# What SyncE waits for at the end of a gated attention and SSM kernel: every transfer's semaphore, or only those not known to have landed

## The chip, the cores and the metric

One Trainium2 chip, one NeuronCore of it. The time is the device time of one execution in microseconds (us); less is better. The profile is of one execution on that core. The engines are TensorE (PE in the profile, its weight loads PEld), VectorE (DVE), ScalarE (ACT), GpSimd (POOL) and SyncE (SP). SyncE does no arithmetic here: it issues transfers (DMAs) and waits on semaphores. Every engine has an instruction queue of its own, and the engines meet only through semaphores.

## What is computed

Two branches work on the same input of 2048 tokens by 512 channels and are mixed by a gate for each token. Branch A is an attention with a compressive memory over four segments of 512 tokens, with 32 heads of 16; branch B is a diagonal state-space layer, a causal convolution of length 2048 for each channel, written with FFTs.

```python
x = A_x
g = _sigmoid((x * gate_w).sum(-1, keepdims=True))
a = _A_ref(x, A_wq, A_wk, A_wv, A_wo, A_beta)
b = _B_ref(x, B_A_re, B_A_im, B_B_re, B_B_im, B_C_re, B_C_im, B_log_dt, B_Dskip)
return g * a + (1 - g) * b
```

The output is 2048 x 512 in bf16, 2 MB.

## The kernel before

The kernel is a graph of operations (`Op`), each with an engine, what it reads and what it writes. A fixed list, `ORDER`, says in which order they are put into the queues; `Sched.replay` walks this list and gives each operation its place `pos` in it, and `Sched.emit` turns it into instructions. At the end of the graph `final(s, tb)` runs 16 times, for four segments of four blocks of 128 tokens. It multiplies the attention's result by the output weights in PSUM, adds the state-space branch on VectorE (line 1389), and sends 128 x 512 values to the output. These 16 transfers are the last ones that SyncE issues.

`emit` works out which waits are needed. The names that matter:

- `dsem` is the list of semaphores for transfers. `NDMA` is 150; GpSimd issues nine transfers, which is not over 20, so `nhw` is 150 - 30 = 120 semaphores for the queues of SyncE and ScalarE, used in turn (`k = nd % nhw`), and nine more, one for each transfer of GpSimd: 129. A transfer adds 16 to its semaphore when it has landed.
- `duse[k]` is the last transfer so far on semaphore `k`, and `dcnt[k]` the number of transfers on it.
- `know` is what an engine can be sure of when it has waited: for each semaphore the highest count that it knows to be reached. An operation starts with what its engine knew (`last[o.eng]`). It waits for another operation only when that isn't known already, and with every wait it takes over all that the other operation's engine knew at that point (`d.know`). `last[e]` keeps the result for the engine's next operation. After the walk, `last["SP"]` is what SyncE knows behind its last transfer.
- `make(e)` writes an engine's queue. For SyncE it appends a loop behind the last transfer (lines 336 to 339): a wait for each semaphore that was ever used, in the order of their numbers, until its full count. All engines then meet at the end of the block (line 1436 in the profile).

The loop doesn't run on the chip: it writes one wait after the other into the program, and the compiler forms instructions from them. In the profile they are the `EVENT_SEMAPHORE` instructions of line 339.

Of the kernel before, what the change touches and what calls it, by code (L numbers as in the profile page):

```python
# [98 lines left out]
class Sched:  # L99
# [164 lines left out]
    def emit(self):  # L264
        nc, es = self.nc, self.es
        sems = {e: es.enter_context(nc.semaphore("q_" + e)) for e in ("PE", "ACT", "DVE", "POOL")}
        npool = sum(o.isdma for o in self.prog["POOL"])
        nhw = NDMA - npool if npool > 20 else NDMA - 30
        dsem = [es.enter_context(nc.semaphore("d%d" % i)) for i in range(nhw + npool)]
        block = es.enter_context(nc.Block())  # L270
        duse = [None] * len(dsem)
        dcnt = [0] * len(dsem)
        nd = nsw = 0
        last = {e: {} for e in self.prog}
        for o in self.order:
            know = dict(last[o.eng])
            o.waits = []
            deps = {id(d): d for d in o.alld}
            if o.isdma:
                if o.eng == "POOL":  # L280
                    k = nhw + nsw
                    nsw += 1
                else:
                    k = nd % nhw
                    nd += 1
                if duse[k] is not None:
                    deps[id(duse[k])] = duse[k]
                duse[k] = o
                dcnt[k] += 1
                o.sem, o.val = ("D", k), dcnt[k]  # L290
            else:
                o.sem, o.val = o.eng, o.idx
            o.inc = False
            for d in sorted(deps.values(), key=lambda d: -d.pos):
                assert d.pos < o.pos
                if d.eng == o.eng and o.eng == "PE":
                    continue
                if know.get(d.sem, 0) >= d.val:
                    continue
                o.waits.append(d)  # L300
                d.inc = True
                for kk, vv in d.know.items():
                    if know.get(kk, 0) < vv:
                        know[kk] = vv
            last[o.eng] = know
            o.know = dict(know)
            o.know[o.sem] = max(o.know.get(o.sem, 0), o.val)
        cum = {}
        for e, lst in self.prog.items():
            n = 0  # L310
            for o in lst:
                if not o.isdma and o.inc:
                    n += 1
                cum[id(o)] = n

        def tok(d):
            if d.isdma:
                return dsem[d.sem[1]], 16 * d.val
            return sems[d.eng], cum[id(d)]

        def make(e):
            def run(eng):
                for o in self.prog[e]:
                    need = {}
                    for d in o.waits:
                        s, v = tok(d)
                        if id(s) not in need or need[id(s)][1] < v:
                            need[id(s)] = (s, v)
                    for s, v in need.values():
                        eng.wait_ge(s, v)  # L330
                    ins = o.fn(eng)
                    if o.isdma:
                        ins.then_inc(dsem[o.sem[1]], 16)
                    elif o.inc:
                        ins.then_inc(sems[e], 1)
                if e == "SP":
                    for k in range(len(dsem)):
                        if dcnt[k]:
                            eng.wait_ge(dsem[k], 16 * dcnt[k])
            return run  # L340
        with nc.allow_low_precision("bf16 kernel by design"):
            block.sync(make("SP"))
            block.tensor(make("PE"))
            block.scalar(make("ACT"))
            block.vector(make("DVE"))
            block.gpsimd(make("POOL"))
# [1135 lines left out]
```

## Time and profile before

| | |
|---|---|
| runs of the kernel before | 301.18, 306.3, 302.49 us |
| their median | 302.49 us |
| the profiled execution | 302.64 us |
| its span, first to last instruction | 300.8 us |
| mean granted TensorE clock in it | 0.985 |
| busy in the span: PE, VectorE, ScalarE | 264.5, 267.1, 261.2 us |
| transfers issued to the output | 16, of 128 KB each |

The span is shorter than the execution's own time by 1.8 us. Rows of one line of the kernel read so: line, engine (a q behind it is the engine's instruction queue), operation and tiles, the count, the shortest, median and longest duration in ns, and the start of the first and the last in us from the span's start. With a window, only the instructions inside it are counted. An instruction that waits for a semaphore has its start where the wait is over, so that the time it waited stands as a gap before it. "DMA to landing" is the time from a transfer's issue to the semaphore's last increment.

### The profile page before, as it was taken

To read this page: it belongs to the slowest core of one execution; us is meant where nothing else is said; L and a number is where in the kernel's file an instruction comes from. 1 tells how busy PE (TensorE), PEld (TensorE's weight loads), DVE (VectorE), ACT (ScalarE), POOL (GpSimd) and SP (SyncE) were. 2 spreads that over 40 slices of the span, in tenths; PEclk is the share of its full clock that TensorE was granted. 3 is DMA by queue.
4 is the path that set the end of the run, shared out by engine and by line. 5 is a ranking of instruction groups with operands and counts; after the bars stand their busy time and mean duration, and the time that the engine had idled before them with its cause. 6 is when DMAs were issued, how large, how long until landed. Compare 5 with 4: busy or idle time off the path is not lost.

```text
span 300.8 us, 10359 instructions
## 1 busy us (share of the span) xinstructions
PE 264.5 (88%) x4358; PEld 185.1 (62%) x4395; DVE 267.1 (89%) x651; ACT 261.2 (87%) x307; POOL 7.8 (3%) x18
## 2 busy tenths in 40 slices
PE   5768677987898989999899889999999999998990
PEld 3434344564556656677666666777766887886540
DVE  2799999989999899989999987999899988969881
ACT  4998999999999999969999989899989899988300
POOL 7000000000010000000000000000000000000000
PEclk9997999999999899999999999999999999999998
DMA  6963364433226535464755568776778777557652
GB/s 157 300 196 97 107 137 128 107 91 89 77 79 176 141 69 172 135 182 125 233 160 167 153 186 245 207 221 208 209 228 224 240 219 228 149 152 197 190 181 68
DMA packets 58865, 49.89 MB, mean 166 GB/s; under 512 B 19569, under 2 KB 54274, under 8 KB 58818
## 3 DMA queue, kind: packets, MB, share of 16 engines
q1 hardware_dynamic: 58096, 48.71, 56.3%
q8 instruction: 35, 0.57, 0.9%
q0 software_dynamic: 288, 0.21, 0.5%
q10 hardware_dynamic: 434, 0.30, 0.4%
q14 instruction: 12, 0.10, 0.1%
HBM read 28.88 MB, written 8.39 MB: 124 GB/s over the span
## 4 chain that ended last, share of the span: by engine, by line
PE 46%; ACT 31%; DVE 8%; DMA 7%; issue 5%; SPq 0%; ACTq 0%
PE psum L699 45%; ACT sb L1095 15%; ACT sb L226 10%; DMA sb<-c_DNM 3%; ACT sb L826 3%; DMA sb<-sb 2%; DMA sb<-in_A_x_dram 2%; DVE sb L227 1%; DVE sb L1389 1%; DVE sb L1327 1%; ACT sb L973 1%; DVE sb L1195 1%; DVE sb L1198 1%; DVE sb L1107 1%; PE psum L970 1%
## 5 line engine op out<-in xcount | busy, mean ns | idle before, releaser
L699 PE MATMUL psum<-sb 128*128 128x17 bf16 (+10 forms) x4224 | 255.2, 225 | 26.9 <-ACT sb L1095 11.5
L699 PEld LDWEIGHTS psum<-sb 128*128 128x128 bf16 (+5 forms) x4261 | 175.4, 99 | 102.5 <-issue 20.9
L1095 ACT ACTIVATE sb<-psum 128x2048 bf16<-128x2048 f32 x80 | 151.9, 1899 | 7.3 <-PE psum L699 6.2
L226 ACT ACTIVATE sb<-psum 128x512 bf16<-128x512 f32 (+3 forms) x162 | 94.7, 640 | 13.9 <-PE psum L699 13.0
L227 DVE CAST sb<-psum 128x512 bf16<-128x512 f32 x60 | 40.9, 691 | 7.1 <-PE psum L699 6.9
L1198 DVE TENSOR_TENSOR sb<-sb 128x512 bf16<-128x512 bf16 (+3 forms) x44 | 24.1, 549 | 1.2 <-PE psum L699 1.0
L1202 DVE TENSOR_TENSOR sb<-sb 128x512 bf16<-128x512 bf16 (+3 forms) x44 | 24.0, 551 | 0.5
L1195 DVE TENSOR_TENSOR sb<-sb 128x512 bf16<-128x512 bf16 (+3 forms) x44 | 24.0, 551 | 0.2
L1107 DVE TENSOR_TENSOR sb<-sb 128x1024 bf16<-128x1024 bf16 (+1 forms) x40 | 22.4, 573 | 1.7 <-ACT sb L1095 1.4
L1327 DVE TENSOR_TENSOR sb<-sb 128x1024 bf16<-128x1024 bf16 x32 | 21.7, 682 | 2.4 <-DMA sb<-sb 2.4
L1070 DVE TENSOR_TENSOR sb<-psum,sb 128x256 bf16<-128x256 f32 x32 | 13.4, 418 | 0.5
L826 ACT ACTIVATE sb<-sb 128x512 f32<-128x512 f32 x18 | 11.9, 659 | 0.1
L1389 DVE SCALAR_TENSOR_TENSOR sb<-sb,psum 128x512 bf16<-128x512 bf16 x16 | 11.1, 742 | 0.9 <-PE psum L699 0.5
L1235 DVE TENSOR_TENSOR sb<-sb 128x2048 bf16<-128x2048 bf16 x8 | 9.4, 1212 | 0.0
L1230 DVE TENSOR_TENSOR sb<-sb 128x4096 bf16<-128x4096 bf16 x4 | 9.1, 2281 | 0.0
L1067 DVE RECIPROCAL sb<-psum 128x16 f32<-128x16 f32 x32 | 7.8, 246 | 1.1 <-PE psum L699 1.1
L1147 DVE TENSOR_TENSOR sb<-psum,sb 128x512 bf16<-128x512 f32 x12 | 8.3, 688 | 0.3
L973 ACT ACTIVATE sb<-psum 128x512 bf16<-128x512 bf16 x12 | 7.4, 624 | 1.1 <-PE psum L970 1.1
L827 DVE TENSOR_TENSOR sb<-sb 128x256 f32<-128x256 f32 x18 | 7.5, 419 | 0.2 <-ACT sb L826 0.2
L1024 ACT ACTIVATE sb<-sb 128x512 bf16<-128x512 bf16 x12 | 7.4, 627 | 0.2 <-PE psum L699 0.2
L828 DVE SCALAR_TENSOR_TENSOR sb<-sb 128x256 f32<-128x256 f32 x18 | 7.5, 415 | 0.0
L835 DVE CAST sb<-sb 128x512 bf16<-128x512 f32 x17 | 7.1, 417 | 0.0
(77 smaller groups left out, 113.8 us busy)
## 6 DMA issues: line engine op xcount, KB each, us to landing
sb<-c_DNM SPq DMA_DIRECT2D x32, 320.0 KB, 3.7
sb<-c_DNM SPq DMA_DIRECT2D x32, 192.0 KB, 3.4
sb<-sb SPq DMA_DIRECT2D x84, 64.0 KB, 3.0
scr_Z<-sb SPq DMA_DIRECT2D x16, 256.0 KB, 2.4
sb<-scr_Z SPq DMA_DIRECT2D x32, 128.0 KB, 3.1
sb<-sb SPq DMA_DIRECT2D x32, 128.0 KB
sb<-in_A_x_dram SPq DMA_DIRECT2D x4, 512.0 KB, 5.3
scr_C<-sb SPq DMA_DIRECT2D x8, 256.0 KB, 3.3
```

The source lines that it names most:

```text
L226: fa = lambda e: e.activation(dst(), src(), ACT.Copy)
L227: fd = lambda e: e.tensor_copy(dst(), src())
L699: mm = lambda e, o_, l, r_, st, sp, **kw: e.matmul(o_, lhsT=l, rhs=r_, start=st, stop=sp, skip_group_check=True, **kw)
L826: op("ACT", ("As", 512), lambda e, sq=sq, Z=Z: e.activation(ap(sq, n=512), ap(Z, n=512), ACT.Square), r=[Z], w=[sq], key=PW[h] + PWS * k)
L1070: op("DVE", ("V1", 256), lambda e: e.tensor_tensor(ap(o1, gi * 16, [[128, 4], [32, 4], [1, 16]]), ap(T, dims=[[68, 4], [17, 4], [1, 16]]), ...
L1095: o = op("ACT", ("Ax", 2048), lambda e, P=P, pT=pT: e.activation(ap(pT, n=2048), ap(P, n=2048), ACT.Exp, scale=0.25), r=[P], w=[pT])
L1107: op("DVE", ("V2", 128 * nb), lambda e, pT=pT, dims=dims: e.tensor_tensor(ap(pT, dims=dims + [[1, 128]]), ap(pT, dims=dims + [[1, 128]]), ...
L1195: op("DVE", ("V2" if n > 1 else "V1", 256 * n), lambda e: e.tensor_tensor(run(tile, ne, dst, 1), run(tile, ne, src, sstep), zz(cl * 512), ...
L1198: op("DVE", ("V2" if n > 1 else "V1", 256 * n), lambda e: e.tensor_tensor(run(t2, n, 0, 1), run(tile, ne, src, sstep), zz(cl * 512 + 256), ...
L1202: op("DVE", ("V2" if n > 1 else "V1", 256 * n), lambda e: e.tensor_tensor(D_(), D_(), ap(t2, n * 128, [[-n * 128, 2], [2 * n, 64], [1, 2 * ...
L1327: op("DVE", ("V2", 1024), lambda e, Y=Y, XAB=XAB, K3=K3: e.tensor_tensor(ap(Y, dims=[[512, 2], [1, 512]]), ap(XAB, dims=[[512, 2], [1, 512 ...
L1389: op("DVE", ("V1", 512), lambda e: e.scalar_tensor_tensor(ap(ou, n=512), ap(CTT[s], tb * 512, n=512), ap(omgT, 4 * s + tb, n=1), ap(P, n=5 ...
```

## The change

Behind SyncE's last transfer, the loop over the semaphores is changed in two ways. It goes through them in the order of the place of the last transfer on each (`duse[k].pos`), the oldest first, with unused semaphores ahead (-1); and it writes a wait only where what SyncE knows, `last["SP"]`, is less than the full count of that semaphore. The old test, `dcnt[k]` not zero, is contained in the new one, since an unused semaphore has a count of 0 and 0 is not less than 0.

```diff
                 if e == "SP":
-                    for k in range(len(dsem)):
-                        if dcnt[k]:
+                    for k in sorted(range(len(dsem)), key=lambda k: duse[k].pos if duse[k] else -1):
+                        if last["SP"].get(("D", k), 0) < dcnt[k]:
                             eng.wait_ge(dsem[k], 16 * dcnt[k])
```

Nothing else is changed: the order of the operations, the semaphores that each transfer uses, and all waits ahead of the loop are the same.

## The prediction

> **What bounds the kernel now.** The page comes first, for the span and for what its last part holds: its head, the clock row of the forty slices and the engines' shares of the chain that ended last.
>
> ```profile
> span 300.8 us, 10359 instructions
> PEclk9997999999999899999999999999999999999998
> PE 46%; ACT 31%; DVE 8%; DMA 7%; issue 5%; SPq 0%; ACTq 0%
> ```
>
> The body is a chain through TensorE and ScalarE, and the change touches none of it. The shares add up to 97%; of the rest, the chain's last piece and a table of stretches at the end show the larger part. In the table each row is a stretch, its length, the busy time of PE, weight loads, VectorE, ScalarE and GpSimd with instruction counts, the granted TensorE clock, the DMA share and the GB/s.
>
> ```profile
> 293.97 0.75 DVE sb L1389
> 290.00:294.80 4.80, 3.88 (x18) 1.57 (x16) 4.41 (x7) 0.00 (x0) 0.00 (x0) 1.00 0.52 172
> 294.80:297.00 2.20, 0.00 (x0) 0.00 (x0) 0.00 (x0) 0.00 (x0) 0.00 (x0) 1.00 0.33 110
> 297.00:299.00 2.00, 0.00 (x0) 0.00 (x0) 0.00 (x0) 0.00 (x0) 0.00 (x0) 0.93 0.02 4
> 299.00:300.80 1.80, 0.00 (x0) 0.00 (x0) 0.00 (x0) 0.00 (x0) 0.00 (x0) 0.50 0.00 0
> ```
>
> The last arithmetic ends at 293.97 + 0.75 = 294.7 us. From there to 300.8 no engine computes: 6.1 us, 2% of the span. Until about 297 data still moves; after that almost nothing does. So the last stretch is neither arithmetic nor transfer, and the views of SyncE's queue have to tell what it is: all output transfers, the last one alone with its time to landing, the waits at line 339 (the loop that the change edits), and who was waited for there (total us, times, longest).
>
> ```profile
> L222 SPq DMA_DIRECT2D out_dram<-sb x16: 332/333/594, 284.0 to 294.7; - x16
> ...
> L222 SPq DMA_DIRECT2D out_dram<-sb x1: 333/333/333, 294.7 to 294.7; - x1
> ...
> DMA to landing us min/median/max: 1.7/1.7/1.7
> ...
> L339 SPq EVENT_SEMAPHORE  x64: 27/28/28, 295.1 to 300.4; - x64
> L339 SPq EVENT_SEMAPHORE  x5: 28/28/28, 295.1 to 295.6; - x5
> L339 SPq EVENT_SEMAPHORE  x59: 27/28/28, 296.5 to 300.4; - x59
> ...
> SPq L339 <- DMA out_dram<-sb: 1.0, 2, 0.8
> ```
>
> The loop became 64 instructions. Two for each would make 128 semaphores; that they hold two each is my reading of 64 against the 129 that the code allots (150 - 30, and one for each of nine GpSimd transfers), the odd one going with the branch behind the loop. Five begin by 295.6. Then SyncE stands still until 296.5, which is when the last transfer, issued at 294.7 and 1.7 us on its way, lands at 296.4; the waits view confirms that output transfers are the only thing SyncE ever stood for here, twice, 1.0 us in all. The sixth instruction therefore is the wait for the last transfer. The 58 behind it wait for transfers that landed long before, and pass at the speed of the queue until 300.4. Nothing else runs then, so they lie bare on the end of the kernel.
>
> **The change part by part.** *What is removed.* The pitch of a wait that doesn't stop comes from a stretch in which all pass, and one irregular place stands in three narrow windows.
>
> ```profile
> L339 SPq EVENT_SEMAPHORE  x33: 28/28/28, 298.0 to 300.0; - x33
> ...
> L339 SPq EVENT_SEMAPHORE  x2: 28/28/28, 297.3 to 297.4; - x2
> nothing on L339; most used: []
> L339 SPq EVENT_SEMAPHORE  x3: 28/28/28, 297.8 to 297.9; - x3
> ```
>
> 33 in 2.0 us is 0.061 us each, twice the 28 ns of the record. 58 x 0.061 = 3.5 us. Between 297.4 and 297.8 SyncE issued nothing: 0.4 us, 0.3 more than a pitch. Together 3.8 us; the difference of first and last start, 300.4 - 296.5 = 3.9, agrees. I take 3.9, because it needs no model of the pitch. It all lies on the path: the end of the program waits for SyncE, as the rows of the block's end show.
>
> ```profile
> L1436 SPq COMPARE_BRANCH  x1: 41/41/41, 300.4 to 300.4; - x1
> L1436 SPq DRAIN  x1: 13/13/13, 300.6 to 300.6; - x1
> L1436 POOLq EVENT_SEMAPHORE  x2: 17/17/17, 300.7 to 300.7; - x2
> L1436 PEldq EVENT_SEMAPHORE  x1: 51/51/51, 300.8 to 300.8; - x1
> ```
>
> Branch, drain, GpSimd's signal and the release of the others follow the loop in 0.4 us, with nothing between; they move forward with it and stay as long.
>
> [...]
>
> *What stays.* The new list holds a semaphore only if SyncE's own bookkeeping hasn't seen its last value. Each wait hands SyncE everything that the engine it waited for knew, and the waits ahead of the last outputs are on VectorE's line 1389, the last step of every chain; so loads that any engine consumed are known. The 16 output transfers are waited for by nobody, so they stay: 16 semaphores, some 8 instructions. I can't see the bookkeeping in the trace, so the count is bounded: 16 from below, all 129 from above. It costs nothing up to a point: SyncE reaches the loop at 295.1 and the last transfer lands at 296.4, and 1.3 us at 0.061 is 21 instructions, 42 semaphores, hidden by the transfer's flight. I take 16, by the row of the 16 outputs and the lack of any other waiting at line 339. Should the cover go, because the list is longer, each pair more costs 0.061 us.
>
> *What moves.* The list is now in order of issue, so the newest output is its end. The compiler may pair the list otherwise; if the wait for the newest came first of eight, seven would follow it, 7 x 0.061 = 0.4 us. If last, none. I take none, for before it was one of the middle of the numbers that came early, and now nothing in the list is newer; 0.4 stays for the range. No transfer is moved, no wait is added, and the queues of GpSimd, ScalarE, VectorE and TensorE get the same instructions; what SyncE issues up to 294.7 is the same too.
>
> *What is late next.* The flight of the last transfer, 1.7 us behind the last addition. It isn't touched.
>
> Sum: the profiled execution took 302.64 us, its span 300.8, with 1.8 outside it that I leave as they are. 302.64 - 3.9 = 298.7; the median of the runs shown, 302.49, is 0.15 below that execution, so the median would be 298.6 to 298.7. New span: 296.9.
>
> **The rivals.** *A fetch behind the branch.* The gap of 0.4 us at 297.4 looks like SyncE waiting for instructions, and one block of instructions was moved in that tail, as the row of the queue between 297 and 300.8 us shows.
>
> ```profile
> q14 instruction: 1, 0.01, 0.9%
> ```
>
> In the changed kernel the branch comes at 296.5, ahead of both. If the code behind the branch isn't there yet, SyncE waits at the branch instead: 0.3 us as in the gap gives 302.64 - 3.6 = 299.0; as long as an output's whole flight, 1.7 us, gives 302.64 - 2.2 = 300.4. Against it: from branch to drain took 0.2 us before, and SyncE stands for nearly a second microsecond at the last transfer, in which a fetch can go on. [...]
>
> *The list isn't short.* If nearly all 129 stay, 64 instructions run from 295.1 without the stop, 64 x 0.061 = 3.9, plus the 0.3 gap, to 299.0 or 299.3; the branch was at 300.4, so 1.1 to 1.4 us are gained: 301.2 to 301.5. For it: nothing in the trace shows the list. Against it: the merging of what each engine knows, above.
>
> *The tail isn't in the measured time, or something of the same length stands behind it.* Then 302.6. Against it: 302.64 and the span differ by only 1.8 us, less than the tail's 3.9, so at least 2.1 of it is counted.
>
> *Slower: stretches at half clock.* Two stretches of the body ran at a granted clock of 0.50, and in the second the chain was on TensorE.
>
> ```profile
> 22.23:25.63 3.40, 3.18 (x11) 1.05 (x8) 3.35 (x11) 3.17 (x4) 0.00 (x0) 0.50 0.47 112
> 97.32:100.72 3.40, 3.25 (x108) 2.18 (x108) 2.32 (x10) 2.88 (x5) 0.00 (x0) 0.50 0.59 148
> 97.28 3.31 PE psum L699 x61
> ```
>
> Such a stretch costs up to half its 3.4 us, 1.7. The tail itself ended at 0.50, idle; a program shorter by 3.9 us starts and ends elsewhere in whatever steps the throttle counts. If the body caught more of them, in the thin stretches beside 22 and 97 us, it would decide from three on: 3 x 1.7 = 5.1 against 3.9, and 298.7 + 5.1 = 303.8. The runs shown, 301.18 to 306.3, differ by just about three. Against it: nothing ties the place of the windows to the tail, and the same instructions at the same distances feed TensorE.
>
> **How the numbers follow.** The forecast, 298.7, has 0.75. The fetch has 0.12 (299.0 to 300.4), the long list 0.06 (301.2 to 301.5), no gain 0.04, slower 0.03. The likeliest case gives the number: 298.7. The range goes down by one half-clock stretch, 298.7 - 1.7 = 297.0, which is also close to the fastest run shown less the gain (301.18 - 3.9 = 297.3), and up to 301.4, through the fetch and into the long list, and over a median that is drawn up by one or two disturbed bodies; left out are no gain, slower, and bodies beyond one stretch. What a measurement of this kernel tells from no change is about 2%, 6 us; the whole bare tail is 3.9, 1.3%, so the gain itself stays within it. Faster by over 2% (under 296.4) needs the tail and two stretches at half clock less, 7.3 us: 0.05. Slower by over 2% (over 308.5) needs six stretches more: 0.02. The rest, 0.93, is within.
>
> **What would show it.** Right: eight or so instructions at line 339, the last beginning when the last output lands, 1.7 us behind its issue; the branch one pitch later; the span ending some 0.5 us behind that landing; the stretch before 294.8 as it was. Wrong list: more than 21 instructions there. Wrong order: several instructions behind the landing. Fetch: a gap between branch and drain of over 0.2 us, or an instruction transfer inside it. Wrong altogether: landing and end as close as that and the time still 302, which would put the tail outside what is measured, or a granted clock row with more low slices.

## The result and the profile after

The changed kernel took 300.29 us, the median of 20 runs (296.87 to 304.84); beside it the kernel before took 304.17 us in 20 runs (300.42 to 309.34). The ratio is 0.9879, with a 95% interval from 0.9839 to 0.9918: 3.7 us less, 2.5 to 4.9 by the interval. All ratios in this document leave out the runs that took over 1.5% longer than the fastest of the same kernel. The difference of the medians, over all 20 runs each, is 3.9 us. The profiled execution of the changed kernel took 298.33 us against 302.64, its span 296.4 against 300.8.

Lines of the page, and then of the views of line 339, of the last output transfer, of the waits of SyncE from 290 us on, and of the block's end, all of the changed kernel:

```profile
span 296.4 us, 10298 instructions
...
PEclk9999999999999999999999999999999999999999
...
q14 instruction: 11, 0.09, 0.1%
```

```profile
L339 SPq EVENT_SEMAPHORE  x3: 17/28/28, 294.7 to 296.0; - x3
...
L222 SPq DMA_DIRECT2D out_dram<-sb x1: 332/332/332, 294.3 to 294.3; - x1
...
DMA to landing us min/median/max: 1.7/1.7/1.7
...
SPq L339 <- DMA out_dram<-sb: 1.2, 2, 0.6
...
L1436 SPq COMPARE_BRANCH  x1: 41/41/41, 296.0 to 296.0; - x1
L1436 SPq DRAIN  x1: 13/13/13, 296.2 to 296.2; - x1
```

61 of the 64 wait instructions are gone, and the count of recorded instructions fell by as many, 10359 - 10298. The last output is issued at 294.3 and lands 1.7 us later, at 296.0; the last of the three waits begins at 296.0, the branch one pitch behind it, the drain 0.2 us behind that, and the span ends at 296.4. The stretches at the end show the same from the side of the engines (stretch, its length, busy PE, weight loads, VectorE, ScalarE and GpSimd, clock, DMA share, GB/s):

```profile
294.20:296.00 1.80, 0.00 (x0) 0.00 (x0) 0.03 (x1) 0.00 (x0) 0.00 (x0) 1.00 0.44 148
296.00:296.40 0.40, 0.00 (x0) 0.00 (x0) 0.00 (x0) 0.00 (x0) 0.00 (x0) 1.00 0.00 0
```

Where 3.8 us passed without arithmetic and with hardly any data before (297.0 to 300.8), 0.4 are left. By the unrounded starts of the trace, the end of the span comes 2.18 us behind the issue of the last output, and came 6.10 us behind it before: 3.92 us. The two spans differ by 4.40 us. The other 0.5 us lie ahead of the last issue, where both kernels run the same instructions, and are of the kind by which runs of one kernel differ: in a second profile of the changed kernel the last output is issued 1.2 us earlier than in this one.

### The profile page after: what moved, and what is told of

Its sections match the earlier page's. It is cut to its first block, busy times and chain, and to the rows that moved or that the text cites. A ratio compares the mean times of both kernels' runs of the same rounds, so it can differ in the third digit from the quotient of the medians.

```text
span 296.4 us, 10298 instructions
## 1 busy us (share of the span) xinstructions
PE 264.6 (89%) x4358; PEld 185.4 (63%) x4395; DVE 266.9 (90%) x651; ACT 261.1 (88%) x307; POOL 7.8 (3%) x18
## 4 chain that ended last, share of the span: by engine, by line
PE 35%; ACT 29%; DVE 15%; DMA 10%; issue 7%; SPq 2%; ACTq 0%; DVEq 0%
PE psum L699 35%; ACT sb L1095 14%; ACT sb L226 9%; DMA sb<-sb 5%; DVE sb L227 3%; ACT sb L826 2%; SPq L222 2%; DMA sb<-in_A_x_dram 2%; DMA sb<-c_DNM 2%; DVE sb L1389 2%; DVE sb L1327 1%; DMA out_dram<-sb 1%; DVE sb L1195 1%; DVE sb L1198 1%; ACT sb L973 1%
```

## The experiments

One distance carries the readings: from the issue of the last output to the end of the span. It leaves out the body, whose time moves by several us from run to run, and it repeats closely: the two profiles of the changed kernel give 2.18 and 2.17 us. All values of it are from the unrounded starts of the traces. The traces also list the semaphores of each instruction: a wait instruction holds two of them, the first only one where the count is even, and one is left for the branch behind the loop. So 6 semaphores make 3 wait instructions, and 129 make 64.

| kernel | semaphores waited for at the end | wait instructions | last issue to end, us | ratio to before (95%) |
|---|---|---|---|---|
| before | 129, by number | 64 | 6.10 | 1 |
| changed | 6, by age | 3 | 2.18 | 0.9879 (0.9839 to 0.9918) |
| sort alone | 129, by age | 64 | 5.09 | 0.998 (0.9939 to 1.0021) |
| list of 36 | 36, by age | 18 | 2.35 | 0.9833 (0.9742 to 0.9924) |
| waits ahead of the outputs | 6, by age | 3 | 2.17 | 0.9883 (0.9831 to 0.9936) |
| loop twice | 258, by number | 129 | 9.02 | 1.0142 (1.0082 to 1.0203) |
| 15 output buffers | 15, by age | 7 | 2.18 | 0.9867 (0.9808 to 0.9925) |
| changed, again | 6, by age | 3 | 2.17 | 0.9885 (0.9814 to 0.9956) |

**The sort alone.** The filter is taken out, the order stays.

```diff
-                        if last["SP"].get(("D", k), 0) < dcnt[k]:
+                        if dcnt[k]:
```

> All 129 semaphores are waited for again, but in order of age. Theory (only waits that begin after the last output has landed cost time): the 64 wait instructions run without a stop from 0.4 us behind the issue of the last output, 64 x 0.061 us and one gap of 0.3, so the end comes 0.4 + 3.9 + 0.3 + 0.5 = 5.1 us behind that issue, where it was 6.1 before the change and 2.2 with it; the time is about 1.0 us below before. Rival (the list's length alone decides): 6.1 us, the time as before. Rival (the order does the work of the change): 2.2 us, 3.9 below before.

Line 339, the last output, and two narrow windows on line 339:

```profile
L339 SPq EVENT_SEMAPHORE  x64: 27/28/28, 295.7 to 300.0; - x64
...
L222 SPq DMA_DIRECT2D out_dram<-sb x1: 332/332/332, 295.3 to 295.3; - x1
...
DMA to landing us min/median/max: 1.7/1.7/1.7
...
L339 SPq EVENT_SEMAPHORE  x3: 28/28/28, 296.9 to 297.3; - x3
nothing on L339; most used: []
```

5.09 us, as the theory had it, and neither the 6.1 nor the 2.2 of the rivals. The newest output is now the last in the queue, and it has landed at 297.0 while SyncE is still at the older ones: the stop of 0.8 us that the kernel before had at its sixth wait is gone. So the flight of the last output hides the waits that run before it lands, 20 of them here (the twentieth begins at 296.95), and those that run after the landing are bare, even though they stand ahead of the wait for that output. The time moved by 0.2%, and the interval holds both the expected 1.0 us and none, but not 3.9. The last window, from 297.0 to 297.3, is empty: the gap of 0.4 us is here too, after the twentieth wait as before.

**A list of 36.** The loop of the change, with the 36 semaphores used last.

```diff
-                    for k in sorted(range(len(dsem)), key=lambda k: duse[k].pos if duse[k] else -1):
-                        if last["SP"].get(("D", k), 0) < dcnt[k]:
+                    for k in sorted(range(len(dsem)), key=lambda k: duse[k].pos if duse[k] else -1)[-36:]:
+                        if dcnt[k]:
```

> The changed loop with 36 semaphores, the 36 that were used last, 30 of them long known to have landed: 18 wait instructions in place of 3. Theory (the flight of the last output hides up to 21 of them): the end 2.2 us behind the issue of the last output, as with the change, and the time 3.9 below before. Rival (each wait costs its 0.061 us wherever it stands): 2.2 + 15 x 0.061 = 3.1 us, 3.0 below before.

Line 339, the last output, and the steps of the block's end in this execution:

```profile
L339 SPq EVENT_SEMAPHORE  x18: 17/28/28, 297.2 to 298.6; - x18
...
L222 SPq DMA_DIRECT2D out_dram<-sb x1: 332/332/332, 296.9 to 296.9; - x1
...
DMA to landing us min/median/max: 1.7/1.7/1.7
...
L1436 SPq DRAIN  x1: 13/13/13, 298.8 to 298.8; - x1
...
L1436 DVEq EVENT_SEMAPHORE  x1: 21/21/21, 299.0 to 299.0; - x1
L1436 PEldq EVENT_SEMAPHORE  x1: 51/51/51, 299.0 to 299.0; - x1
L1436 SPq EVENT_SEMAPHORE  x1: 17/17/17, 299.2 to 299.2; - x1
```

The eighteenth wait begins at 298.6, when the output of 296.9 lands: fifteen more waits moved it by nothing, so the rival falls. Yet the distance is 2.35, 0.17 more than with the change, and the rows say where: all engines are released at 299.0, SyncE itself only at 299.2, 0.4 us behind its drain instead of 0.16. In the kernel before, in the sort alone, with the loop twice and with the waits ahead of the outputs, SyncE's gap of 0.4 us always lies between the same two of its recorded instructions, the 335th and the 336th. In this kernel these are the drain and SyncE's last step. The times, of four runs, are too few to tell 3.9 us from 3.0.

**The same waits in another place.** The change stays, and waits for the 128 semaphores whose counts SyncE knows by then (those that the outputs use again, up to the use before) are put ahead of the first output transfer. 126 of them make 63 wait instructions.

```diff
                 for o in self.prog[e]:
+                    if e == "SP" and o is self.prog["SP"][-16]:
+                        for (d, k), v in sorted((x, v) for x, v in o.know.items() if isinstance(x, tuple) and x != o.sem):
+                            eng.wait_ge(dsem[k], 16 * v)
```

> The loop of the change at the end, and the waits that it leaves out put ahead of the first output transfer, where SyncE stood idle for 5.5 us in the profile of before: as many instructions as before the change, in another place. Theory (the place decides): they take about 4 us of the idle time there, the first output is issued when it was, the end comes 2.2 us behind the issue of the last output, and the time is 3.9 below before. Rival (the instructions cost what they cost, by their number and by having to be fetched): the time as before, the 4 us appear ahead of the outputs.

The head of the page, the added waits (line 326 of this kernel), the waits at its end (line 342) and its outputs, all and the last:

```profile
span 296.6 us, 10399 instructions
...
L326 SPq EVENT_SEMAPHORE  x63: 27/28/178, 277.7 to 282.1; - x63
...
L342 SPq EVENT_SEMAPHORE  x3: 17/27/28, 294.8 to 296.1; - x3
...
L222 SPq DMA_DIRECT2D out_dram<-sb x16: 332/384/1705, 283.6 to 294.4; - x16
...
L222 SPq DMA_DIRECT2D out_dram<-sb x1: 333/333/333, 294.4 to 294.4; - x1
```

63 waits take 4.4 us, from 277.7 to 282.1, where SyncE has nothing to do, and the first output goes out at 283.6 (284.0 before, 283.3 with the change). With 64 instructions more in SyncE's queue than the changed kernel has (385 recorded against 321), the span is 296.6 against 296.4, and the ratio to before is that of the change, 0.9883 against 0.9879. The number of instructions costs nothing here; their place does.

**The loop twice.** The kernel before, with its loop run two times.

```diff
-                    for k in range(len(dsem)):
-                        if dcnt[k]:
-                            eng.wait_ge(dsem[k], 16 * dcnt[k])
+                    for h in range(2):
+                        for k in range(len(dsem)):
+                            if dcnt[k]:
+                                eng.wait_ge(dsem[k], 16 * dcnt[k])
```

> The loop of before, gone through twice: 258 semaphores, 129 wait instructions. The wait for the newest output stands only behind some 70 others, so nothing stops. Theory: 0.4 + 129 x 0.061 + 0.3 (a gap, perhaps two) + 0.5 = 9.1 to 9.4 us from the issue of the last output to the end, against 6.1: 3.0 to 3.3 us more time than before. Rival (no wait is hidden by the flight): 6.1 + 65 x 0.061 = 10.1 us, 4.0 more. Rival (the tail lies outside the measured time): a longer tail in the profile, the time as before.

The loop (line 340 of this kernel) and its last output:

```profile
L340 SPq EVENT_SEMAPHORE  x129: 17/28/28, 294.4 to 302.6; - x129
...
L222 SPq DMA_DIRECT2D out_dram<-sb x1: 332/332/332, 294.0 to 294.0; - x1
```

129 instructions from 294.4 to 302.6 with one gap are 0.061 us each, and the distance is 9.02 us: 0.4 + 129 x 0.061 + 0.3 + 0.5 = 9.1, with one gap. It is 2.9 us longer than before, not 4.0, because the stop at the last output is gone here too. The time rose by 1.4% (0.8 to 2.0%), 2.5 to 6.1 us: a longer tail is in the measured time.

**Fifteen output buffers.** The filter keeps only what SyncE doesn't know. Printed for the changed kernel, its list is this, as semaphore and place of its last transfer in the order:

```
d65 1832   d66 1835   d67 1839   d68 1843   d69 1848   d70 1849
```

The 16 outputs have d55 to d70, and the trace of the changed kernel has the same six, d65 to d70, in its three waits and its branch. Six stay and ten are known, and the bookkeeping shows from where: the output tiles lie in six buffers, so VectorE waits for the landing of the output that was in a buffer before it writes the next one into it (its wait for d64 at place 1847, for example), and SyncE, which waits for VectorE, learns it. The same list shows that the sort changes nothing here: the six stand in the order of their numbers already, so the filter alone would write the same waits. To test the cause, 15 buffers are used, in room that is free by then, each output tile the next one.

```diff
+        nou = 0
...
-    ouP = mkpool("ou", 1024, 6, 3)
+    ouP = mkpool("ou", 1024, 15, 3)
...
-                    T.pool.take(T, next(slots))
+                    k = next(slots)
+                    if not T.isp and T.pool.name == "ou":
+                        k, nou = nou % 15, nou + 1
+                    T.pool.take(T, k)
```

> The changed kernel with 15 output buffers in place of 6, so that VectorE waits for the landing of one output instead of ten, and SyncE learns of one landing instead of ten: the list at the end grows from 6 semaphores to 15, from 3 wait instructions to 7. Theory (the list's length is set by how many outputs VectorE had to wait for; up to 21 instructions are hidden): 7 instructions, the end still 2.2 us behind the issue of the last output. VectorE's idle time before line 1389 that output landings ended, 0.5 us in the profile of the changed kernel, goes; the time is 3.9 to 4.4 us below before. Rival (longer list costs): 4 x 0.061 = 0.2 us more behind the last issue. Rival (the reuse of buffers cost nothing, since TensorE or the additions bound the last stage anyway): the last addition ends when it did, 3.9 below before.

The change ran once more in the same series.

> The changed kernel itself, on the chip and beside the runs of the kernel with 15 buffers, to compare the two and to see how far its own body moves from run to run. Theory: 3 wait instructions, the end 2.2 us behind the issue of the last output in this execution too, the time 3.9 us below before; what differs from the first profile lies ahead of the last issue. Rival (part of the first profile's gain came from the tail by chance, such as a quick landing): another distance than 2.2.

First the changed kernel's first profile, then its second one, then that with 15 buffers: all outputs, what VectorE waited for in the last stage, and in the last fence the waits of SyncE at the end (line 343 there).

```profile
L222 SPq DMA_DIRECT2D out_dram<-sb x16: 332/332/447, 283.3 to 294.3; - x16
...
DVE sb L1389 <- DMA out_dram<-sb: 0.5, 1, 0.5
```

```profile
span 295.2 us, 10298 instructions
...
PEclk9579999999999999999999999999999999999999
...
L222 SPq DMA_DIRECT2D out_dram<-sb x16: 332/392/1382, 282.3 to 293.0; - x16
...
DVE sb L1389 <- DMA out_dram<-sb: 0.2, 1, 0.2
```

```profile
L222 SPq DMA_DIRECT2D out_dram<-sb x16: 332/432/1502, 285.6 to 296.3; - x16
...
L343 SPq EVENT_SEMAPHORE  x7: 27/28/28, 296.7 to 298.0; - x7
...
DVE sb L1393 <- PE psum L703: 0.5, 1, 0.5
```

Seven waits in place of three, and the distance at the end is 2.18 us, the same: the cause of the list's length is shown, and that a list of 15 costs no more than one of 6. The changed kernel's second profile gives 2.17 again, so the first one's end was no chance. VectorE's wait for output landings is gone from its list of waits with 15 buffers; but with six it comes and goes too, for the profiles of the kernel before and of the sort alone have none. What it was worth is little: the last stage, from the first output to the last, takes 10.7 us with 15 buffers, 11.0 and 10.7 with six. In time the two, 298.88 and 299.54 us of six runs each, can't be told apart (0.9867 and 0.9885 with intervals that cover each other). No version beats the change by what can be measured.

## Why the prediction was right

- *What lies bare behind the last landing.* Right, and the term of the sum was right: 3.9 us forecast, 3.92 measured in the tail. The times agree but say less: 3.9 us between the medians, 2.5 to 4.9 by the interval of the ratio. 298.7 us was forecast beside an execution of 302.64; that the profiled execution of the changed kernel took 298.33 is in part luck, for its body happened to be 0.5 us shorter, and other runs of the same kernel took up to 304.84. The median of 20 runs is 1.6 us above the number, because the three runs known of the kernel before had a lower median, 302.49, than the 20 beside the change, 304.17.
- *The pitch of 0.061 us.* Right from 18 to 129 instructions, and so is the reading that an instruction holds two semaphores: the loop twice adds 65 instructions for 129 semaphores, and 61 ns pass for two of them.
- *What hides a longer list.* Right, by the lists of 36 and 15; the sort alone, with 64 instructions, shows the other side: 20 of them begin before the output lands, where 21 were worked out. No list between 18 and 64 instructions was run.
- *"The 16 output transfers are waited for by nobody, so they stay."* Wrong: six stay. VectorE waits for ten of them, when it writes into a buffer again. The step took the lack of a waiter in SyncE's queue for the lack of any waiter; the wait on VectorE had cost nothing in the profile of before and so had no row. So the lower bound of 16 was wrong too. The mistake was free, since lists of 3, 7 and 18 instructions pass within the flight: the cover saved the number, not the count.
- *The order.* Right that the newest ends the list: the third wait holds d70 with d66, and only the branch follows it, with d65, landed at 293.4. But the sort does nothing in this kernel, which the prediction didn't see. All of the gain is the filter's: it alone would write the same six waits in the same order.
- *What stays of the end, and what is late next.* Right: landing to end took 0.5 us, and the flight 1.7 us, in both profiles of the change.
- *The fetch behind the branch.* Not in the changed kernel: from branch to drain it took the same 0.2 us, and SyncE's program there ends with its 321st recorded instruction, 14 ahead of the place of the gap. The gap can fall into the block's end, though: the list of 36 has it there and pays 0.17 us for it, less than the 0.3 of the rival, since the rest of the gap lies beside the release of the other engines. What SyncE waits for in the gap stays open: the prediction read it together with the one instruction transfer of that tail, but this begins only behind the gap, as the last section shows. The gap follows the count of instructions here, 335 ahead of it in each kernel that has it, and not the branch. That it is a change from one block of instructions to the next was not shown: the transfers of the queue q14 were 8 KB each (0.09 MB in 11), and no run shows how many instructions a block holds.
- *The list isn't short.* Not so; its price was tested by the sort alone, 1.0 us gained against 1.1 to 1.4 worked out.
- *The tail outside the measured time.* Refuted by the medians and by the loop twice.
- *Stretches at half clock.* They come and go without the change: the first profile of the change has none in its body, its second has 10.2 us at half clock, from 8.2 to 18.4 us (slices 2 and 3 of its clock row), and that one has the shorter span, 295.2. So 1.7 us for 3.4 is an upper end, and there they cost little. Over the 20 runs of the change, time and granted clock go together, but loosely: the five runs at 0.999 or more took 296.9 to 298.7 us, the four at 0.987 or less 300.5 to 304.8, and one at 0.988 took 298.1. What makes up the rest of the scatter stays open.

## What to carry to other kernels

Waits that are sure to pass still take their place in the queue, 61 ns here for an instruction with two of them, and at the end of this program nothing else ran beside them: so look at what stands between the landing of the last output and the end of the span. Drop the waits that are known to pass, or put them where the engine idles anyway; as long as the rest passed during the flight of the last transfer, 1.7 us, its length didn't matter here, with the newest at its end in each of these runs: 2.17 and 2.18 us from the last issue to the end with 3 instructions, 2.18 with 7, and 2.35 with 18, where the gap of 0.4 us fell into the block's end. When you ask which transfers somebody already waits for, ask it of every engine: the reuse of a buffer is a wait too, even when it costs nothing and so has no row in the profile.

## What the runs showed that was not expected

SyncE pauses for 0.4 us between its 335th and 336th recorded instruction in each of the five kernels that are long enough, wherever these stand: in the tail before, in the idle stretch ahead of the outputs, or in the block's end. It isn't the time of an instruction transfer. The DMA row of the kernel before, from 297 to 300.8 us in 40 slices, shows when the one of that tail ran:

```profile
DMA  0000000000000030000000000000000000000000
```

It began at 298.4, 0.64 us after SyncE had gone on at 297.8. In the other four kernels with the gap, too, an instruction transfer begins behind it and not in it, by 0.65 us in three and 1.04 us in the one with the waits ahead of the outputs. So the two may belong together, but SyncE doesn't stand there until that transfer lands.

And two of the wait instructions' columns mislead when read alone: a duration of 28 ns stands for a pitch of 61, and the order in which the waits run is not that of the loop that wrote them, since the sixth of 64 was that for d70, the 71st in the list. The traces show the order: it starts in the middle of the list and takes one semaphore from each side, d65 with d64, then d66 with d63, and so on, so that the newest comes last only where it stands at an end of the list.
